# Pole-table products of an S4 convolution: one 96-row group of products, or two 48-row halves in the upper and lower half of the array

## The chip, the cores and the metric

The kernel runs on one core of one Trainium2 chip. The metric is the device time of one execution in microseconds; lower is better. The times shown are medians over several executions of the same program. The profile is one execution taken by the hardware profiler; its span runs from the first instruction to the last.

## The reference

The reference is a block of two mixers on 2048 tokens of 576 channels: an S4 state-space convolution, then a gated MLP with a spatial product. Both are wrapped in adaptive layer norm. What matters here is how the convolution's kernel K comes about, from 128 complex poles for each channel:

```python
dt = jnp.exp(log_dt)[:, None]
A = A_re + 1j * A_im
Bc = B_re + 1j * B_im
Cc = C_re + 1j * C_im
logdA = dt * A
dB = dt * Bc
P = jnp.exp(logdA[:, :, None] * l[None, None, :])
K = jnp.einsum("dn,dnl,dn->dl", Cc, P, dB).real
...
y = irfft(rfft(u padded) * rfft(K padded)) + u * Dskip
...
x = x + ga * y                       # first mixer, on the layer norm of x
x = x + gb * gMLP(layernorm(x) ...)  # second mixer
```

So for each channel and pole a power of exp(dt A) is needed at 2048 positions l, weighted by C dB and summed over the poles. (The lines with the transforms are written shorter here.)

## The kernel before, in words

**Powers as products of tables.** A position is split as l = a + 32 b. A power is then a table over 32 values of a times a table over 64 values of b. Log magnitude and phase of each table entry are linear in the pole's parameters, so TensorE makes them: the parameters of 16 channels, each split into three bf16 parts, stand as the rows of a stationary operand (`lb`, `lc`, `la`), and constant selection rows (`sel`) stream past. Its columns are 16 channels x 32 positions, 512 for one product. `lb` holds the log magnitudes: 3 parts of alpha and 3 of the log weight, times 16 channels, 96 rows. `lc` holds 3 parts of the phase step tau, 48 rows. `la` holds 3 parts of 64 tau (taken modulo 1) and 3 of the phase offset, 96 rows. The 128 output partitions are the poles.

**Groups and ticks.** The 576 channels are 36 groups of 16, `g`, in four chunks of nine. The loop at lines 650 to 714 has 40 ticks; a tick works on several groups at different steps of a pipeline:

- `e_unit` (lines 416 to 426): two products into a `ps` buffer (two PSUM banks, two such buffers) and one into a `pk` bank (four of those), then ScalarE's Exp on each (lines 423 and 426). It is issued for three groups at a time, in every third tick. The table `et` has five buffers.
- `t_unit` (428 to 438): two products into a `ps` buffer, `lc` (line 432) and `la` (433). ScalarE adds a large constant, which rounds (434); VectorE subtracts to get the phase modulo 1 (435) and takes its absolute value (437).
- `s_unit` (440 to 443), one tick later: ScalarE's two Sins, cosine and sine.
- `p_unit` (445 to 459), two ticks later: VectorE's five products of magnitudes with cosines and sines.
- `kg_unit` (461 to 471), three ticks later: 32 small products sum over the poles, and ScalarE copies the result into `kab`; `d_unit` adds the skip term; `k1_unit` (477 to 492), a tick later, takes the first step of K's transform, and ScalarE or VectorE copies it out.

From tick 11 on the same ticks also carry the transform of the input and the product with K's transform: `u_unit` (523 to 532; ScalarE copies `ue`), `z_unit` (534 to 543), `v_unit` (545 to 552; ScalarE copies `v`), and `y_unit` (587 to 597). In ticks 0 to 7 they carry the layer norm and the first step of the input's transform (`ln_unit`, 393 to 408), which uses `ps` buffers too. Behind the ticks come the second norm and the gMLP, whose instructions are mostly recorded at line 140.

**Exp and Sin.** The two functions are not in one table set of ScalarE; where one follows the other the program has an ACT_TABLE_LOAD, at the line of the function that needs it. Copies and the rounding need none.

**How the pole parameters get there.** `poles` (188 to 279) works them out on VectorE and ScalarE, chunk 0 first, chunks 1 to 3 together. `split3` (197 to 213) splits each into three bf16 parts and stores them into the DRAM tensors `pa_d`, `pb_d` and `pc_d`, through GpSimd's (POOL's) DMA queue: five stores for a chunk. `poles_load` (283 to 287) reads the three tables of a chunk back, one DMA each, before tick 0 and in ticks 7, 13 and 21.

**What sets the order.** Within the ticks the instructions are not pinned: a list scheduler orders them for each engine when the program is built, by its own estimates, by priority in order of issue, and by which buffers are free. Startup, tick 0's products and everything behind the ticks are pinned to program order.

Of the kernel before, what the change touches and what calls it, by code (L numbers as in the profile page):

```python
# [11 lines left out]
BF = mybir.dt.bfloat16  # L12
# [19 lines left out]
def consts():  # L32
# [51 lines left out]
    eye = np.eye(16)  # L84
    rgt = np.zeros((6, 16, 16, 32))
    rge = np.zeros((6, 16, 16, 32))
    rpe = np.zeros((6, 16, 16, 64))
# [5 lines left out]
    rpt = np.zeros((6, 16, 16, 32))  # L93
# [59 lines left out]
def ssm(tc, I, x1_d, consts_s, dram, mod_d, mlp):  # L153
# [5 lines left out]
    with ExitStack() as ctx:  # L159
# [23 lines left out]
        sel = tb.tile([96, 2560], BF, name="sel", bufs=1)  # L183
# [4 lines left out]
        def poles(c0, c1, Q, own=None):  # L188
# [8 lines left out]
            def split3(*items):  # L197

                n = 3 // (c1 - c0)
                parts = []  # L200
                for i, (src, dst, k) in enumerate(items):
                    if not todo:
                        t_ = ep.tile([128, 3, 432], BF, name="pt")
                        todo.extend(t_[:, :, w * j:w * j + w] for j in range(n))
                    parts.append((src, dst, k, todo.pop(0), t("sq%d" % (i % 2))))
                for src, dst, k, pt, q in parts:
                    A.activation(pt[:, 0], src, AF.Copy)
                    V.tensor_tensor(q, src, pt[:, 0], op=ALU.subtract)
# [11 lines left out]
            def run():  # L220
# [36 lines left out]
                split3((al, pb_d, 0), (tau, pc_d, 0))  # L257
# [3 lines left out]
                split3((tau64, pa_d, 0), (lw, pb_d, 3))  # L261
# [15 lines left out]
                split3((ph, pa_d, 3))  # L277
# [138 lines left out]
        def e_unit(g):  # L416
            c, gi = divmod(g, 9)
            lb = lt["lb", c]
            e = et[g] = tb.tile([128, 1536], F32, name="et", bufs=5)
            pa = ps2()  # L420
            for h in range(2):
                T.matmul(pa[:, h], lb[:, gi], sel[:, 1024 + 512 * h:1536 + 512 * h], start=True, stop=True)
            A.activation(e[:, :1024].rearrange("p (h n) -> p h n", h=2), pa, AF.Exp)
            pb = ps1()
            T.matmul(pb, lb[:, gi], sel[:, 512:1024], start=True, stop=True)
            A.activation(e[:, 1024:], pb, AF.Exp)

        def t_unit(g):
# [3 lines left out]
            T.matmul(pa[:, 0], lt["lc", c][:, gi], sel[:48, 2048:2560], start=True, stop=True)  # L432
            T.matmul(pa[:, 1], lt["la", c][:, gi], sel[:, :512], start=True, stop=True)
# [11 lines left out]
        def p_unit(g):  # L445
# [6 lines left out]
            c3 = ct.rearrange("p x (c j) -> p x c j", c=16)  # L452
            s3 = f.rearrange("p x (c j) -> p x c j", c=16)
# [1693 lines left out]
```

## Time and profile before

| | |
|---|---|
| median of 3 executions | 1782.84 us (1781.9 to 1785.29) |
| the profiled execution | 1788.13 us |
| its span | 1786.3 us |
| mean granted TensorE clock | 0.978 |
| TensorE (PE) busy | 1686.7 us, 94% |
| VectorE (DVE) busy | 1266.6 us, 71% |
| ScalarE (ACT) busy | 854.4 us, 48% |
| GpSimd (POOL) busy | 227.0 us, 13% |

Times in the profile are in microseconds from the span's start, unless they are marked ns. PE is TensorE's products, PEld its weight loads. A row of the timeline has the start, the duration, the engine, the line of the kernel, the operation, the tile written and the tiles read, shapes, and in brackets how long the engine had been idle and what ended that. A row of the windows has one stretch: its length, and each engine's busy time with the number of instructions. A busy PE is not PE at its peak, since products are pipelined and their ends are modelled.

### The profile page before, as it was taken

How to read it: one execution, taken by the hardware profiler on the slowest of the kernel's cores; microseconds unless marked ns; L12 is line 12 of the kernel's file. 1: busy time of each engine (PE TensorE's matmuls, PEld its weight loads, DVE VectorE, ACT ScalarE, POOL GpSimd, SP SyncE). 2: the span in 40 equal slices, each digit the busy share in tenths (PEclk: the TensorE clock that was granted, in tenths of full speed). 3: DMA queues.
4: the chain of work that ended last, by engine and by line, in shares of the span. 5: the costliest groups of instructions: out<-in, count | busy, mean ns of one | idle time of the engine just before them, and what ended most of it. 6: DMA issues, size and time to landing. Idle time of an engine off the chain costs nothing.

```text
span 1786.3 us, 35743 instructions
## 1 busy us (share of the span) xinstructions
PE 1686.7 (94%) x14830; PEld 1255.3 (70%) x14830; DVE 1266.6 (71%) x2331; ACT 854.4 (48%) x1129; POOL 227.0 (13%) x364
## 2 busy tenths in 40 slices
PE   3599899998899999999989999999999999999999
PEld 1355555565455445777878888888888888888887
DVE  6785999966998998688889677688344468344432
ACT  4778999954477666445434444234222224122210
POOL 2111223332122211000000000000111100111100
PEclk9789999998999999999999999999999999999999
DMA  9465646679688779777665886773766573556531
GB/s 268 145 198 179 196 120 167 176 204 304 206 260 266 249 228 264 284 248 250 240 209 164 282 299 233 269 253 118 250 225 226 203 231 100 193 195 215 194 111 40
DMA packets 182193, 377.80 MB, mean 212 GB/s; under 512 B 37680, under 2 KB 101552, under 8 KB 181264
## 3 DMA queue, kind: packets, MB, share of 16 engines
q1 hardware_dynamic: 140000, 177.29, 33.1%
q0 software_dynamic: 36128, 171.57, 28.9%
q10 hardware_dynamic: 5904, 26.67, 3.7%
q8 instruction: 116, 1.90, 0.4%
q14 instruction: 45, 0.37, 0.1%
HBM read 264.73 MB, written 101.31 MB: 205 GB/s over the span
## 4 chain that ended last, share of the span: by engine, by line
PE 58%; DVE 10%; DMA 8%; issue 4%; ACT 1%; POOL 1%; SPq 0%; ACTq 0%; DVEq 0%; POOLq 0%
PE ps L140 54%; DMA zset<-set_d 2%; DMA wsst<-in_w_spT 1%; DVE zset L140 1%; DVE bsz L140 1%; DMA win_d<-wso 1%; DVE n L140 1%; DVE gt L140 1%; DVE rq L140 1%; PE pk L527 1%; ACT z L140 1%; PE pk L540 1%; DMA ue<-v_d 1%; DMA z_d<-z 1%; DVE wsp L140 1%
## 5 line engine op out<-in xcount | busy, mean ns | idle before, releaser
L140 PEld LDWEIGHTS <-zset 128*128 128x128 f16 x7182 | 702.8, 98 | 95.3 <-DVE zset L140 9.5
L140 PE MATMUL ps<-wsp,zset 128*128 128x256 f16 x6048 | 669.2, 273 | 9.1 <-DVE zset L140 7.5
L140 PE MATMUL pz<-wz,nt 128*128 128x512 f16 (+1 forms) x1120 | 222.5, 358 | 12.3 <-ACT nt L140 5.3
L140 ACT ACTIVATE z<-gt 128x1024 f16<-128x1024 f32 x56 | 59.0, 1054 | 285.4 <-DVE gt L140 285.4
L140 PEld LDWEIGHTS <-nt 128*128 128x128 f16 x1120 | 108.7, 98 | 119.9 <-ACT nt L140 6.9
L140 DVE SCALAR_TENSOR_TENSOR gt<-ps,sc,bsp 128x512 f32<-128x512 f32 x36 | 27.0, 750 | 206.0 <-PE ps L140 204.3
L140 PE MATMUL ps<-wout,z 128*128 128x288 f16 x1344 | 170.0, 286 | 0.0
L1855 POOL DMA_DIRECT2D zset<-set_d x96 | 50.9, 530 | 872.0 <-PE ps L140 626.1
L140 PEld LDWEIGHTS <-z 128*128 128x128 f16 x1344 | 131.5, 98 | 33.0
L140 DVE TENSOR_TENSOR raw<-raw 128x512 f32<-128x512 f32 (+2 forms) x228 | 119.1, 528 | 13.0 <-DMA raw<-z_d 8.7
L140 PE MATMUL ps<-n2o,zset 128*128 128x256 f16 x1134 | 128.2, 273 | 0.0
L140 DVE SCALAR_TENSOR_TENSOR gt<-ps,sc,gt 128x512 f32<-128x512 f32 (+1 forms) x180 | 122.2, 696 | 7.6
L140 ACT ACTIVATE zset<-raw 128x1792 f16<-128x1792 f32 x48 | 81.2, 1691 | 60.8 <-PE ps L140 27.0
L140 DVE TENSOR_TENSOR zset<-raw,zset 128x1792 f16<-128x1792 f32 x48 | 97.0, 2020 | 15.6 <-ACT zset L140 15.6
L140 DVE TENSOR_TENSOR z<-ps,z 128x512 f32<-128x512 f32 (+1 forms) x126 | 72.0, 599 | 36.8 <-ACT z L140 26.7
L140 ACT ACTIVATE wsp<-raw,sc 128x1792 f16<-128x1792 f32 x25 | 44.6, 1784 | 42.7 <-DVE raw L140 35.0
L140 ACT ACTIVATE z<-z,sc 128x1024 f32<-128x1024 f32 x21 | 24.1, 1148 | 75.6 <-DVE z L140 71.9
L435 DVE SCALAR_TENSOR_TENSOR ft<-ft,ps 128x1024 f32<-128x1024 f32 x36 | 43.8, 1217 | 18.0 <-ACT ft L434 18.0
L140 ACT ACTIVATE z<-z,nm,r 128x1152 f32<-128x1152 f32 x24 | 31.4, 1341 | 51.6 <-DVE nm L140 29.5
L140 ACT ACTIVATE z<-pz,sc 128x512 f32<-128x512 f32 (+1 forms) x96 | 51.6, 583 | 9.2 <-PE pz L140 4.6
L140 PE MATMUL ps<-n2q,wf 128*128 128x512 f16 x252 | 55.7, 379 | 0.0
L140 PE MATMUL ps<-wout,z1b 128*128 128x288 f16 x384 | 52.4, 286 | 0.0
(361 smaller groups left out, 2512.0 us busy)
## 6 DMA issues: line engine op xcount, KB each, us to landing
zset<-set_d POOLq DMA_DIRECT2D x96, 896.0 KB, 5.0
raw<-z_d SPq DMA_DIRECT2D x48, 512.0 KB, 5.6
set_d<-zset ACTq DMA_DIRECT2D x24, 896.0 KB, 6.1
z_d<-z POOLq DMA_DIRECT2D x32, 576.0 KB, 9.4
zset<-wa_d POOLq DMA_DIRECT2D x18, 896.0 KB, 4.9
raw<-in_w_spT SPq DMA_DIRECT2D x25, 512.0 KB, 4.5
set_d<-zset SPq DMA_DIRECT2D x12, 896.0 KB, 5.2
u_d<-st1o POOLq DMA_DIRECT2D x16, 576.0 KB, 3.8
```

The source lines that it names most:

```text
L140: return self.tc.keep_in_program_order(f(*a, **k))
L435: V.scalar_tensor_tensor(f, f, MAGIC, pa, op0=ALU.subtract, op1=ALU.subtract)
L527: T.matmul(pm, fwd, u1, start=True, stop=True)
L540: T.matmul(pm[:, w * j:w * j + w], cst[k // 8][:, k % 8], k1t[c][:, k, :w], start=True, stop=True)
L1855: self.nc.gpsimd.dma_start(o, self.set_d[f, j - 1] if j else self.wa_d[f])
```

## The change

A group's 16 channels are split into two halves of eight. The rows of a half, 6 x 8 = 48, stand on partitions 0 to 47 or 64 to 111 of the stationary tiles and of `sel`, so that one half's product runs on the array's upper rows and the other's on its lower rows, each with a PSUM bank of its own. `lc` becomes a 48-row half as well: it is read from `pa_d`, which now holds tau, 64 tau and the offset in nine rows, and the rows of 64 tau meet zeros in `sel`. `pc_d` is gone.

In `e_unit` three products of 512 columns become two of 512 and two of 256, and the second pair goes into a second `ps` buffer, where a `pk` bank was used. In `t_unit` two products of 512 columns become four of 256, each written into runs of 32 columns. Its tables then lie in another order, and `p_unit` reads cosines and sines in runs of 32 elements. Each store of the split parameters becomes two DMAs, and each load too.

```diff
@@ consts
-    eye = np.eye(16)
+    eye = np.eye(8)
...
-    sel = np.concatenate([rgt.reshape(96, 512), rge.reshape(96, 512), rpe.reshape(96, 1024), rpt.reshape(96, 512)], axis=1)
+    half = np.concatenate([rgt.reshape(48, 256), rge.reshape(48, 256), rpe.reshape(48, 512), rpt.reshape(48, 256)], axis=1)
+    sel = np.zeros((112, 1280))
+    sel[:48] = sel[64:] = half
@@ ssm
-        pa_d = dram.tile([4, 6, CW], BF, name="pa_d")
-        pb_d = dram.tile([4, 6, CW], BF, name="pb_d")
-        pc_d = dram.tile([4, 3, CW], BF, name="pc_d")
+        pa_d = dram.tile([4, 2, 9, CW // 2], BF, name="pa_d")
+        pb_d = dram.tile([4, 2, 6, CW // 2], BF, name="pb_d")
...
@@ split3
-                        Q.dma_start(dst[c, k:k + 3].rearrange("q (p f) -> p q f", p=128), pt[:, :, 144 * (c - c0):144 * (c - c0) + 144])
+                        for h in range(2):
+                            Q.dma_start(dst[c, h, k:k + 3].rearrange("q (p f) -> p q f", p=64),
+                                        pt[64 * h:64 * h + 64, :, 144 * (c - c0):144 * (c - c0) + 144])
...
@@ poles_load
-            for n, d_, k in (("lb", pb_d, 6), ("lc", pc_d, 3), ("la", pa_d, 6)):
-                t_ = tb.tile([16 * k, 9, 128], BF, name=n)
-                Q.dma_start(t_, d_[c].rearrange("q (c g n) -> (q c) g n", c=16, g=9))
+            for n, d_, k in (("lb", pb_d, 0), ("lc", pa_d, 0), ("la", pa_d, 3)):
+                t_ = tb.tile([112, 9, 128], BF, name=n)
+                for h in range(2):
+                    Q.dma_start(t_[64 * h:64 * h + 48], d_[c, h, k:k + 6].rearrange("q (c g n) -> (q c) g n", c=8, g=9))
                 lt[n, c] = t_
+
+        def rows(c0, w):
+            return [sel[64 * h:64 * h + 48, c0:c0 + w] for h in range(2)]
+
+        def halves(t, gi):
+            return [t[64 * h:64 * h + 48, gi] for h in range(2)]
@@ e_unit
-            pa = ps2()
-            for h in range(2):
-                T.matmul(pa[:, h], lb[:, gi], sel[:, 1024 + 512 * h:1536 + 512 * h], start=True, stop=True)
+            pa, pb = ps2(), ps2()
+            for h, (l, r) in enumerate(zip(halves(lb, gi), rows(512, 512))):
+                T.matmul(pa[:, h], l, r, start=True, stop=True)
+            for h, (l, r) in enumerate(zip(halves(lb, gi), rows(256, 256))):
+                T.matmul(pb[:, h, :256], l, r, start=True, stop=True)
             A.activation(e[:, :1024].rearrange("p (h n) -> p h n", h=2), pa, AF.Exp)
-            pb = ps1()
-            T.matmul(pb, lb[:, gi], sel[:, 512:1024], start=True, stop=True)
-            A.activation(e[:, 1024:], pb, AF.Exp)
+            A.activation(e[:, 1024:].rearrange("p (h n) -> p h n", h=2), pb[:, :, :256], AF.Exp)
@@ t_unit
-            T.matmul(pa[:, 0], lt["lc", c][:, gi], sel[:48, 2048:2560], start=True, stop=True)
-            T.matmul(pa[:, 1], lt["la", c][:, gi], sel[:, :512], start=True, stop=True)
+            for k, (n, c0) in enumerate((("lc", 1024), ("la", 0))):
+                for h, (l, r) in enumerate(zip(halves(lt[n, c], gi), rows(c0, 256))):
+                    T.matmul(pa[:, h].rearrange("p (c k j) -> p k c j", c=8, k=2)[:, k], l, r, start=True, stop=True)
@@ p_unit
-            c3 = ct.rearrange("p x (c j) -> p x c j", c=16)
-            s3 = f.rearrange("p x (c j) -> p x c j", c=16)
+            c3, s3 = [x.rearrange("p h (c k j) -> p k (h c) j", c=8, k=2) for x in (ct, f)]
```

More of the change, by code (lines that the diff above doesn't have):

```diff
@@ L83, in consts @@
         st3b[rows, 1::2] = tr
-    eye = np.eye(16)
-    rgt = np.zeros((6, 16, 16, 32))
-    rge = np.zeros((6, 16, 16, 32))
-    rpe = np.zeros((6, 16, 16, 64))
+    eye = np.eye(8)
+    rgt = np.zeros((6, 8, 8, 32))
+    rge = np.zeros((6, 8, 8, 32))
+    rpe = np.zeros((6, 8, 8, 64))
     rgt[:3] = eye[None, :, :, None] * a
@@ L92, in consts @@
     rpe[:3] = eye[None, :, :, None] * b
-    rpt = np.zeros((6, 16, 16, 32))
+    rpt = np.zeros((6, 8, 8, 32))
     rpt[:3] = eye[None, :, :, None] * (np.arange(32) + 0.5)
-    sel = np.concatenate([rgt.reshape(96, 512), rge.reshape(96, 512), rpe.reshape(96, 1024), rpt.reshape(96, 512)], axis=1)
+    half = np.concatenate([rgt.reshape(48, 256), rge.reshape(48, 256), rpe.reshape(48, 512), rpt.reshape(48, 256)], axis=1)
+    sel = np.zeros((112, 1280))
+    sel[:48] = sel[64:] = half
     ones = np.zeros((128, 128))
@@ L182, in ssm @@
         tb = tabs.enter_context(tc.tile_pool(name="tb", reuse_waits="tile", bufs=2))
-        sel = tb.tile([96, 2560], BF, name="sel", bufs=1)
+        sel = tb.tile([112, 1280], BF, name="sel", bufs=1)
         dsk = tb.tile([128, 144], F32, name="dsk", bufs=1)
@@ L256, in run @@
                 yield
-                split3((al, pb_d, 0), (tau, pc_d, 0))
+                split3((al, pb_d, 0), (tau, pa_d, 0))
                 yield
@@ L260, in run @@
                 V.tensor_tensor(lw, lw, ldt, op=ALU.add)
-                split3((tau64, pa_d, 0), (lw, pb_d, 3))
+                split3((tau64, pa_d, 3), (lw, pb_d, 3))
                 yield
@@ L276, in run @@
                 V.tensor_tensor(ph, ph, rnd, op=ALU.subtract)
-                split3((ph, pa_d, 3))
+                split3((ph, pa_d, 6))
             return run()
```

## The prediction, made before the changed kernel was run

> **What bounds the kernel now.** I read the page's slices first, to see where the touched code runs. The products of the pole tables belong to ticks 0 to 35, between 44 and 365 us of the 1786.3 us span, slices 2 to 8 of 40.
>
> ```profile
> PE   3599899998899999999989999999999999999999
> DVE  6785999966998998688889677688344468344432
> ACT  4778999954477666445434444234222224122210
> ```
>
> In slices 5 to 8 all three engines stand at 9: whichever gets more work there makes the kernel longer. Averages hide which one has room, so next I asked for the stretches between the starts of the Exp bursts in the full ticks (each burst serves three ticks; columns: PE, weight loads, DVE, ACT, POOL busy, granted clock, DMA share, GB/s).
>
> ```profile
> 189.36:212.44 23.08, 22.80 (x311) 12.79 (x311) 21.34 (x33) 22.52 (x30) 6.76 (x12) 1.00 0.72 202
> 212.44:235.86 23.42, 22.67 (x309) 12.93 (x306) 21.64 (x34) 21.89 (x29) 6.39 (x11) 1.00 0.37 108
> 235.86:257.13 21.27, 20.75 (x293) 11.99 (x293) 19.10 (x30) 21.01 (x28) 4.80 (x8) 1.00 0.33 91
> 257.13:281.42 24.29, 23.54 (x325) 13.87 (x322) 23.61 (x37) 21.88 (x28) 8.72 (x15) 1.00 0.60 173
> 281.42:303.79 22.37, 21.85 (x309) 12.77 (x309) 19.86 (x30) 21.30 (x27) 5.43 (x9) 1.00 0.57 155
> 303.79:328.93 25.14, 24.39 (x341) 14.76 (x338) 23.80 (x38) 21.91 (x29) 8.03 (x13) 1.00 0.62 173
> 328.93:355.21 26.28, 25.76 (x336) 15.02 (x335) 23.77 (x36) 24.59 (x31) 9.02 (x15) 1.00 0.63 176
> sum 165.85, PE 161.75 PEld 94.15 DVE 153.11 ACT 155.11 POOL 49.14; mean PE 23.11 PEld 13.45 DVE 21.87 ACT 22.16 POOL 7.02
> ```
>
> Seven stretches, 21 ticks, 165.85 us. PE is busy 161.75 of them, ACT 155.11, DVE 153.11. So PE sets the pace, but ACT has only 165.85 - 155.11 = **10.74 us** to spare in all 21 ticks, 0.51 us a tick. The third view is the timeline of ACT through one burst and the tick behind it.
>
> ```profile
> 281.42 1.28 ACT L423 ACT_TABLE_LOAD   x1
> 282.72 1.02 ACT L423 ACTIVATE et<-ps 128x1024 f32<-128x1024 f32 x1
> 283.64 0.59 ACT L426 ACTIVATE et<-pk 128x512 f32<-128x512 f32 x1
> 284.11 1.03 ACT L423 ACTIVATE et<-ps 128x1024 f32<-128x1024 f32 x1
> ...
> 286.99 1.11 ACT L434 ACTIVATE ft<-ps,consts_s 128x1024 f32<-128x1024 f32 x1
> 288.12 1.28 ACT L442 ACT_TABLE_LOAD   x1
> 289.42 1.15 ACT L442 ACTIVATE ft<-ft,consts_s 128x1024 f32<-128x1024 f32 x1
> 290.48 1.04 ACT L443 ACTIVATE ft<-ft 128x1024 f32<-128x1024 f32 x1
> 291.42 0.58 ACT L551 ACTIVATE v<-pk 128x512 f32<-128x512 f32 x1
> 291.90 0.64 ACT L471 ACTIVATE kab<-pk 128x256 f32<-128x256 f32 x1
> 292.31 0.66 ACT L528 ACTIVATE ue<-pk 128x512 f32<-128x512 f32 x1
> 292.84 1.12 ACT L434 ACTIVATE ft<-ps,consts_s 128x1024 f32<-128x1024 f32 x1
> ```
>
> A burst costs a table load for Exp (1.28 us), the three units' Exps with no Sin between them, and a table load back for Sin. The steps from start to start are what ACT pays when it never waits: 0.92 us for the wide Exp, 0.47 for the narrow one, about 1.0 for the rounding (L434), 1.06 and 0.94 for the Sins, 0.48, 0.41 and 0.53 for the three copies.
>
> **The change part by part.**
>
> *The order on ACT.* The two Exps of a unit used to read one two-bank `ps` buffer and one `pk` bank; now both read `ps` buffers, of which there are two. Three units in a row therefore need six turns of a ring of two, where they needed three. The scheduler answers to that, and the order in which the instructions stand in the changed program shows how. One letter per ACT instruction, * a table load, E and e the wide and the narrow Exp, t the rounding, s and S the Sins, v g u k copies; six ticks of before, then of after:
>
> ```
> * E e E e E e t * s S v g u k t s S v g u t s S v g u k * E e E e E e t * s S v g u t s S v g u k t s S v g u
> * E e * s * E e * S * E e v g u t k t * s S v g u t s S * E v g u k e E e * s * E e * S t v g u v t s S g u k t s S v g u
> ```
>
> Exp and Sin now alternate inside the burst: six table loads in the first three ticks and four in the next, where there were two and two. Over the whole program I count 58 loads against 32, **26 more**. Of these 20 fall into the seven stretches above (4, 6, 4, 6, 4, 6, 4 = 34 against 14) and 6 into ticks before them; the last burst and the tail have as many as before.
>
> *Full ticks.* 20 x 1.283 us = 25.7 us; 155.11 + 25.7 = 180.8 us of ACT work in stretches that took 165.85. ACT becomes the bound, and the sum without a single wait is +14.9 us. Then I walked by hand through the six ticks with the steps above. In the three-tick group with six loads, the third unit's Exp ends 12.8 us in; the next product on PE needs that buffer and waits some 4 us for it, which costs nothing by itself, since ACT has five instructions of cover. Two roundings then come close together, and the Sin behind them waits for DVE's two steps on the first rounding (1.22 + 0.69 us, with one more in between), about 1.2 us beyond ACT's own time:
>
> ```profile
> 288.14 1.22 DVE L435 SCALAR_TENSOR_TENSOR ft<-ft,ps 128x1024 f32<-128x1024 f32 x1 [2.19 <-ACT ft L434]
> 289.39 0.69 DVE L437 TENSOR_SCALAR ft<-ft 128x1024 int32<-128x1024 int32 x1
> ```
>
> The group with four loads shows no such wait. Three groups of the first kind: 3 x 1.2 = 3.6. **Full ticks: 14.9 + 3.6 = +18.5 us.** Lower end: packed back to back, ACT's steps (with 1.42 us per load, as an instruction ahead of a load does not overlap it) sum to 25.9 and 24.6 us for the two groups, 3 x 25.9 + 4 x 24.6 = 176.1, or +10. Upper end: ACT keeps the idle share that it has now, 180.8 x 165.85 / 155.11 = 193.3, or +27.5.
>
> The Trainium skill has another price: "ScalarE: Activation LUTs", under "What ACT_TABLE_LOAD costs", puts a drain of about 1380 ns on top of 1283 ns, some 2.66 us per switch. Here the load at 281.42 is followed by its Exp at 282.72, 1.30 us on, and no drain shows, so the sum goes by the row.
>
> *Early ticks.* Six more loads, 7.7 us, where ACT has more room.
>
> ```profile
> 55.10:95.20 40.10, 28.02 (x143) 15.31 (x142) 31.08 (x72) 31.55 (x46) 8.68 (x12) 0.73 0.40 131
> 95.20:139.10 43.90, 39.59 (x412) 23.27 (x412) 33.95 (x86) 32.08 (x43) 8.51 (x13) 0.92 0.69 214
> 139.10:164.90 25.80, 21.56 (x301) 13.24 (x300) 16.59 (x28) 23.23 (x32) 4.48 (x7) 1.00 0.44 154
> 164.90:189.36 24.46, 20.38 (x256) 11.16 (x254) 16.97 (x25) 20.72 (x25) 2.07 (x4) 0.72 0.86 258
> ```
>
> ACT is busy 107.6 of 134.3 us, 80%, and no engine is full; the layer norm's products share the `ps` ring. I take half of the 7.7, **+4 us**; the ends are 0, and 14 if all loads show and the ring, now with 12 more turns there, costs another 0.5 us a turn.
>
> *PE.* Per unit before: three 96-row products, then a 48-row and a 96-row one.
>
> ```profile
> 281.13 0.38 PE L425 MATMUL pk<-sel,lb 96*128 96x512 bf16 x1
> 281.35 0.59 PE L422 MATMUL ps<-sel,lb 96*128 96x512 bf16 x2
> ...
> 286.20 0.39 PE L432 MATMUL ps<-sel,lc 48*128 48x512 bf16 x1
> 286.52 0.39 PE L433 MATMUL ps<-sel,la 96*128 96x512 bf16 x1
> ```
>
> Products of one shape step by 0.22 us; where the row count changes the step is 0.32. A unit is 3 x 0.22 + 2 x 0.32 = 1.3 us. After: two of 512 and two of 256 columns, then four of 256, each on half the rows. No row shows two halves side by side. If they run so, a unit is about 0.22 + 0.11 + 0.22 plus two changes of 0.1, 0.75 us, a gain of 0.55; if one after another with every weight load showing (0.1 each, eight), 2.1 us, a loss of 0.8. In 21 ticks that is -11.6 to +16.8, so PE's work is between 150.2 and 178.6 us: below ACT's 180.8 at both ends. I take **0** on the path. The cover is ACT's new work; without that cover PE's gain would be the kernel's.
>
> *DVE and the wider patterns.* Its cosines and sines are now read in runs of 32 elements 64 apart. The nearest rows are a copy into runs 128 elements apart and a product on dense data:
>
> ```profile
> 290.06 0.69 DVE L490 COPY k<-pk 128x512 f32<-128x512 f32 x1
> 290.67 0.68 DVE L454 TENSOR_TENSOR pg<-et,ft 128x512 f32<-128x512 f32 x1
> ```
>
> No difference: **0**.
>
> *DMAs.* Stores of the split poles go from 20 to 40 and loads from 12 to 24, all on POOL's queue, 0.76 and 0.52 us of POOL each. The first tables hurry most:
>
> ```profile
> 26.21 0.52 POOL L140 DMA_DIRECT2D la<-pa_d  x1 [0.55 <-DMA pa_d<-pt]
> ...
> 44.26 1.06 PE L140 MATMUL ps<-sel,lb 96*128 96x512 bf16 x2
> ```
>
> Five more stores and three more loads put at most 5 x 0.76 + 3 x 0.52 = 5.4 us ahead of the last load; the first product starts 18 us behind it, after the modulation's products on PE. **0**, at most 1.
>
> **Sum.** 18.5 + 4 = +22.5 us. The profiled execution took 1788.13 us, 1.83 over its span; the median of the three timed runs is 1782.84, 5.3 us lower, and the addition is carried over to it: 1782.84 + 22.5 = **1805**. Behind tick 36 the transforms, the second norm and the gMLP hang on the last tick, so I pass the delay on undiminished.
>
> **The rivals.**
> - *Packed* (1793): ACT runs back to back and the early loads hide, +10. For it: ACT has work of several ticks queued. Against: the Sins' wait on DVE.
> - *Halves in line* (1811): the two halves don't run side by side, so the change doesn't do what it says. PE at up to 178.6 us is then within 2 us of ACT and the two make each other wait; I put 6 us on it, a third of PE's extra.
> - *ACT keeps its idle share and the ring costs early* (1824): 27.5 + 14 = +41.
> - *PE's gain decides* (1772): faster. PE sets the pace today, and 21 x 0.55 = 11.6 us less of it is 11 us less of kernel, if the 20 loads fit into ACT's 10.74 us of room. That decides at 0.54 us a load; the row has 1.28. A balance in between gives no change (1783).
> - *The skill's drain* (1833): a stall of another 1.38 us behind each load, 20 x 2.66 = 53, less 10.74, +42, and 8 early. The page is the one named above; the rows speak against it.
>
> **How the numbers follow.** Forecast 50%, packed 15%, halves in line 15%, idle share kept 12%, PE's gain 4%, no change 3%, the drain 1%. The range takes in the first four: 1793 to 1824. A measurement here can tell about 0.2%, 3.6 us, from no change: slower 93%, same 3%, faster 4%.
>
> **What would show it.** In the profile after: 26 more table loads, ACT busier by about 33 us in all; ACT at 95% or more in the full ticks, their six-tick period near 52.7 us in place of 47.4; PE below 93% there, waiting for `ps` buffers on the Exps; the pair of half products stepping by one product's time or by two. It is wrong if the full ticks keep their length, or if they grow with ACT idle and PE full.

## The result, and the profile after

| | before | after |
|---|---|---|
| median of 4 executions each | 1784.07 us (1781.9 to 1786.35) | 1824.83 us (1821.32 to 1831.69) |
| ratio after/before | | 1.023 (95%: 1.0212 to 1.0247) |
| the profiled execution, its span | 1788.13, 1786.3 us | 1826.31, 1824.5 us |
| mean granted TensorE clock | 0.978 | 0.964 |

The change costs 40.8 us by the medians. The forecast was +22.5, and the range ended at 1824. The profiled span grew by 38.2 us. After's slices, to lay over those of before:

```profile
PE   4586788899799999999999999999999999999999
DVE  6774778885798999788899777689444469344432
ACT  5767999983567666545544343334222124122110
PEclk8688889999899999999999999999999999999999
```

In slices 5 to 8 ACT stands at 9; PE, which stood at 8 or 9 there before, at 7 and 8. The granted clock (PEclk) is at 6 to 8 in the first six slices.

The second view answers to before's stretches between Exp bursts (columns as there).

```profile
205.67:230.00 24.33, 22.00 (x301) 11.66 (x300) 20.78 (x31) 24.07 (x31) 8.18 (x15) 0.93 0.44 116
230.00:258.56 28.56, 22.33 (x290) 12.27 (x289) 21.06 (x33) 26.49 (x30) 5.13 (x9) 0.82 0.29 82
258.56:283.23 24.67, 22.27 (x323) 12.95 (x322) 21.37 (x32) 24.56 (x31) 4.91 (x9) 1.00 0.35 98
283.23:308.84 25.61, 19.73 (x240) 11.80 (x239) 18.92 (x30) 25.10 (x28) 7.91 (x15) 0.87 0.41 121
308.84:336.42 27.58, 26.30 (x409) 15.39 (x409) 24.35 (x37) 25.87 (x34) 6.86 (x12) 1.00 0.56 162
336.42:362.74 26.32, 21.14 (x256) 12.52 (x253) 19.52 (x31) 25.09 (x28) 5.73 (x10) 0.87 0.47 132
362.74:394.78 32.04, 30.73 (x438) 17.96 (x437) 28.05 (x43) 29.02 (x38) 10.06 (x18) 1.00 0.62 175
sum 189.11, PE 164.50 PEld 94.56 DVE 154.05 ACT 180.19 POOL 48.77; mean PE 23.50 PEld 13.51 DVE 22.01 ACT 25.74 POOL 6.97
```

189.11 us where before had 165.85: **+23.3**. ACT is busy 180.19 us, 95% of it, and idle 8.9; PE was idle 4.1 us and is now idle 24.6. The groups with six loads (the second, fourth and sixth row) run at a clock of 0.82 to 0.87, and the work that PE does not get done there comes later: in the last group PE is the full engine (30.73 of 32.04).

The same view for the ticks ahead of them, cut at the first products or bursts that answer to before's cuts.

```profile
53.61:94.27 40.66, 26.54 (x156) 15.42 (x155) 33.73 (x79) 29.02 (x45) 13.81 (x22) 0.73 0.42 138
94.27:142.71 48.44, 42.24 (x480) 25.75 (x482) 33.34 (x84) 34.58 (x45) 7.65 (x12) 0.89 0.59 182
142.71:178.71 36.00, 22.98 (x306) 14.75 (x307) 16.52 (x26) 30.28 (x36) 5.99 (x10) 0.80 0.35 119
178.71:205.67 26.96, 18.95 (x229) 11.47 (x230) 15.56 (x23) 23.04 (x28) 2.77 (x5) 0.70 1.05 304
sum 152.06, PE 110.72 PEld 67.40 DVE 99.16 ACT 116.92 POOL 30.23; mean PE 27.68 PEld 16.85 DVE 24.79 ACT 29.23 POOL 7.56
```

Before took 134.26 us from its first rounding (55.10) to its first full burst (189.36); after takes 152.06: **+17.8**. More than half of it is in the third row, which begins with a burst: 36.00 in place of 25.80 us, or 34.92 if the row ends, as before's does, at the next burst's table load (177.63). ACT is not full there, PE is busy 64%, DVE 46%, and the clock is 0.80 where it was 1.00. In the four rows together PE idles 41.3 us where it idled 24.7, and its waits for an Exp to free a `ps` buffer add up to 14.5 us where before had 0.4. The three longest kinds in after (us in total, times, longest):

```profile
PE ps L432 <- ACT et L435: 4.9, 3, 4.0
...
PE ps L415 <- ACT et L435: 4.3, 1, 4.3
...
PE ps L444 <- ACT et L435: 2.8, 1, 2.8
```

The start-up is 1.5 us shorter and what is behind the ticks 1.4 us: 17.8 + 23.3 - 1.5 - 1.4 = 38.2.

**One early burst on two engines.** ACT first. The same burst of before began at 139.13 and its last Exp ended at 144.75, 5.6 us.

```profile
142.71 1.28 ACT L435 ACT_TABLE_LOAD   x1
144.01 1.02 ACT L435 ACTIVATE et<-ps 128x1024 f32<-128x1024 f32 x1
144.93 0.59 ACT L436 ACTIVATE et<-ps 128x512 f32<-128x512 f32 x1
145.54 1.28 ACT L453 ACT_TABLE_LOAD   x1
146.83 1.15 ACT L453 ACTIVATE ft<-ft,consts_s 128x1024 f32<-128x1024 f32 x1
148.00 1.28 ACT L435 ACT_TABLE_LOAD   x1
149.29 1.02 ACT L435 ACTIVATE et<-ps 128x1024 f32<-128x1024 f32 x1
...
153.19 1.28 ACT L435 ACT_TABLE_LOAD   x1
154.48 1.02 ACT L435 ACTIVATE et<-ps 128x1024 f32<-128x1024 f32 x1
155.40 0.59 ACT L436 ACTIVATE et<-ps 128x512 f32<-128x512 f32 x1
```

It now takes 142.71 to 155.99, 13.3 us: two Sins and four more loads stand between the Exps. ACT is never idle in it. PE, in the same time:

```profile
140.93 0.28 PE L444 MATMUL ps<-sel,lc 48*128 48x256 bf16 x2
141.05 0.27 PE L444 MATMUL ps<-sel,la 48*128 48x256 bf16 x2
...
141.74 0.39 PE L432 MATMUL ps<-sel,lb 48*128 48x512 bf16 x2
...
144.04 0.28 PE L434 MATMUL ps<-sel,lb 48*128 48x256 bf16 x2
...
145.08 0.39 PE L432 MATMUL ps<-sel,lb 48*128 48x512 bf16 x2 [0.18 <-ACT et L435]
145.57 0.28 PE L434 MATMUL ps<-sel,lb 48*128 48x256 bf16 x2
...
150.37 0.61 PE L432 MATMUL ps<-sel,lb 48*128 48x512 bf16 x2 [4.05 <-ACT et L435]
150.85 0.39 PE L434 MATMUL ps<-sel,lb 48*128 48x256 bf16 x2
155.56 0.40 PE L415 MATMUL ps<-gsp,cs 96*128 96x288 bf16 x1 [4.31 <-ACT et L435]
155.75 1.16 PE L416 MATMUL ps<-ln_x,rt 128*128 128x288 f32 x2
...
161.34 0.65 PE L416 MATMUL ps<-ln_x,rt 128*128 128x288 f32 x2
```

The third unit's product stands idle 4.05 us for the buffer that ACT's Exp at 149.29 frees, and the layer norm's product behind it 4.31 us for the next one. No other product runs on PE in either wait. The granted clock falls from 1.00 to 0.50 at 147.3 us, in the first wait, 0.9 us after PE's last product: the wide pair takes 0.61 us at 150.37 where it took 0.39 at 145.08. It is back at 1.00 at 160.9, 5.3 us after the products go on; until then the layer norm's pair takes 1.16 us in place of 0.65. The Trainium skill, "TensorE: Matmul & The Clock Gate", section "What's actually happening", says that the clock falls to half after an idle window of about 3.4 us and comes back after a busy one. The trace agrees in kind, but not in the time: here 0.9 us without a product come before the fall.

The loads by line, in after's first 460 us, and what waited longest in its seven full stretches:

```profile
L435 ACT ACT_TABLE_LOAD x25 | 32.1, 1283 | 0.4
L453 ACT ACT_TABLE_LOAD x16 | 20.5, 1283 | 0.3
L454 ACT ACT_TABLE_LOAD x10 | 12.8, 1283 | 0.2
```

```profile
PE ps L444 <- ACT et L435: 14.5, 4, 4.4
...
DVE et L466 <- ACT ft L454: 8.9, 4, 2.4
```

58 loads in the whole program against 32, as the order had shown. PE's four waits are of phase products (L444) that want the buffer of an Exp: 4.42 us in each of the three six-load groups, and one of 1.25. DVE's four are for Sins that come late. One of PE's, and what PE does after it:

```profile
242.84 0.40 PE L444 MATMUL ps<-sel,lc 48*128 48x256 bf16 x2 [4.42 <-ACT et L435]
...
246.36 2.08 PE L559 MATMUL pk<-za,small 128*128 128x512 f32 x2
...
254.87 1.02 PE L559 MATMUL pk<-za,small 128*128 128x512 f32 x2
```

Held 4.42 us, then 2.08 us for a pair that takes 1.02 at 254.87. The granted clock is 0.50 from 239.4 to 249.7.

### The profile page after: what moved, and what is told of

It reads as the page before. It is cut to its first block, busy times and chain, and to the rows that moved or that the text cites. A ratio compares the mean times of both kernels' runs of the same rounds, so it can differ in the third digit from the quotient of the medians.

```text
span 1824.5 us, 36040 instructions
## 1 busy us (share of the span) xinstructions
PE 1688.5 (93%) x14938; PEld 1257.4 (69%) x14938; DVE 1268.5 (70%) x2331; ACT 889.2 (49%) x1155; POOL 239.4 (13%) x396
## 4 chain that ended last, share of the span: by engine, by line
PE 57%; DVE 11%; issue 4%; DMA 4%; ACT 1%; POOL 1%; ACTq 0%; POOLq 0%; DVEq 0%
PE ps L142 53%; PE pz L142 2%; DMA zset<-set_d 2%; DVE bsz L142 1%; DVE zset L142 1%; DVE n L142 1%; DVE rq L142 1%; DMA z_d<-z 1%; DVE gt L142 1%; DVE wsp L142 1%; ACT z L142 1%; DVE nt L142 0%; DVE rx L142 0%; DVE wso L142 0%; DVE z L142 0%
```

## The experiments

Two questions: which part of the change costs the time (the halves on PE, or the sixth turn of the `ps` ring), and by which way a table load of 1.28 us becomes more. The table puts the runs side by side. A burst runs from its first wide Exp, with the table load where one stands directly ahead of it, to the end of its last Exp, read from ACT's timeline and added up over the three early bursts (those of ticks 3, 6 and 9) and over the seven full ones. A narrow Exp that the scheduler has drawn ahead of its burst, with a load of its own, is not counted (before has one at 81.02 us and one at 164.87). "Start" is the start of the first full burst, "stretches" the length of the seven; both are of one profiled execution, which lay 9 us above its kernel's median in e1, 4 above in before and e9, 4.5 below in e10, and within 3 us in the others. The median is that of the kernel, the ratio that to before on the same chip with its 95% interval.

| kernel | loads | early bursts | start | full bursts | stretches | median | ratio |
|---|---|---|---|---|---|---|---|
| before | 32 | 17.6 | 189.36 | 40.8 | 165.85 | 1784.07 | |
| after | 58 | 38.7 | 205.67 | 84.7 | 189.11 | 1824.83 | 1.023 (1.0212 to 1.0247) |
| e1 ring alone | 58 | 42.5 | 209.53 | 86.2 | 191.43 | 1826.06 | 1.0238 (1.0214 to 1.0262) |
| e5 halves, old banks | 34 | 15.0 | 180.96 | 40.6 | 164.37 | 1778.5 | 0.9958 (0.9938 to 0.9977) |
| e4 halves in `t_unit` | 32 | 20.6 | 186.07 | 41.7 | 165.25 | 1784.74 | 0.9994 (0.9979 to 1.0009) |
| e6 after, no loads | 8 | 25.3 | 189.50 | 45.9 | 157.85 | 1775.75 | 0.9942 (0.9926 to 0.9958) |
| e7 before, no loads | 8 | 13.9 | 178.96 | 32.2 | 160.81 | 1774.57 | 0.9929 (0.9912 to 0.9946) |
| e3 loads between the Sins | 58 | 18.4 | 189.69 | 40.3 | 170.67 | 1794.89 | 1.0061 (1.004 to 1.0082) |
| e11 loads in the burst | 54 | 25.3 | 192.97 | 69.7 | 192.21 | 1818.72 | 1.019 (1.0174 to 1.0206) |
| e8 ring early | 40 | 40.4 | 205.87 | 44.8 | 167.20 | 1806.37 | 1.0117 (1.01 to 1.0134) |
| e13 after, tables early | 60 | 36.5 | 201.76 | 85.4 | 195.58 | 1825.35 | 1.0227 (1.0203 to 1.0251) |
| e14 before, tables early | 32 | 17.8 | 182.73 | 40.8 | 165.82 | 1782.19 | 0.9994 (0.9977 to 1.0011) |
| e9 after, Exps together | 36 | 31.7 | 214.57 | 48.6 | 162.17 | 1807.62 | 1.0122 (1.0103 to 1.0141) |
| e10 before, Exps together | 34 | 25.0 | 192.14 | 39.9 | 162.72 | 1794.2 | 1.0056 (1.0037 to 1.0075) |
| e12 ring late, together | 34 | 15.0 | 184.06 | 48.7 | 163.55 | 1776.49 | 0.995 (0.9934 to 0.9966) |
| e2 halves in `pk` banks | 32 | 16.3 | 189.02 | 41.6 | 193.32 | 1817.96 | 1.0186 (1.0168 to 1.0204) |
| e16 two `pk` turns | 32 | 18.3 | 189.18 | 41.6 | 191.02 | 1809.52 | 1.0145 (1.0119 to 1.0171) |
| e15 e5, tables early | 34 | 15.0 | 182.12 | 40.6 | 164.37 | 1773.77 | 0.9943 (0.9922 to 0.9963) |

### The ring or the halves: e1, e5, e4

e1 is before with the narrow product in a `ps` buffer, so six turns and no halves.

```diff
-            pb = ps1()
+            pb = ps2()[:, 0]
```

> The kernel before with one edit: the narrow product of e_unit goes into a ps buffer in place of a pk bank. No halves, no more DMAs. Its program has 58 table loads, like the changed kernel, and the three-unit Exp burst is cut by Sins in the same way. Theory RING (six turns on a ring of two ps buffers make the loss: the table loads, and PE held behind a waiting product): about the changed kernel's time, 1815 to 1835 us. Theory HALVES (the half products, their weight loads, mode changes or DMAs make the loss): at most a few us over the kernel before, 1784 to 1795.

The whole loss is there, without a single half: +40.6 us by the medians, 58 loads, 20.2 us more ahead of the first full burst and 25.6 in the stretches. The additional turns of the ring are the cause.

e5 is the reverse, after with the halves and the old banks: the two wide half products stay, and the narrow one is one product of all 112 rows (those between the halves hold zeros) into one `pk` bank.

```diff
+                if n == "lb":
+                    G.memset(t_[32:64], 0.0)
...
-            pa, pb = ps2(), ps2()
+            pa = ps2()
...
+            pb = ps1()
+            T.matmul(pb, lb[:, gi], sel[:, 1024:], start=True, stop=True)
+            A.activation(e[:, 1024:], pb, AF.Exp)
```

> The changed kernel with PSUM used as before: the wide products of e_unit and all products of t_unit in halves, but the narrow one is one product over all 112 rows (the 16 between the halves are zero) into one pk bank. Three ps turns and three pk turns per burst, 34 table loads (two more than before). The DMAs are those of the changed kernel. Theory TURNS (any additional turn of a PSUM ring in the burst holds PE, the halves themselves cost nothing): 1778 to 1790 us. If halves or DMAs had a price of their own: over 1795.

Faster than before by 0.4%. Its window over the seven stretches:

```profile
180.96:345.33 164.37, 154.19 (x2242) 91.53 (x2242) 153.13 (x232) 154.69 (x200) 49.11 (x81) 1.00 0.53 150
```

PE is busy 154.19 us in place of 161.75: the halves do take 7.6 us of work off it. The stretches get only 1.5 us shorter; the rest of the gain is ahead of them.

e4 has the halves in `t_unit` alone (the parameter tables `la` and `lc` and their stores and loads as in the change, `lb` as before):

```diff
-            T.matmul(pa[:, 0], lt["lc", c][:, gi], sel[:48, 2048:2560], start=True, stop=True)
-            T.matmul(pa[:, 1], lt["la", c][:, gi], sel[:, :512], start=True, stop=True)
+            for k, (n, c0) in enumerate((("lc", 256), ("la", 0))):
+                for h, (l, r) in enumerate(zip(halves(lt[n, c], gi), rows(c0, 256))):
+                    T.matmul(pa[:, h].rearrange("p (c k j) -> p k c j", c=8, k=2)[:, k], l, r, start=True, stop=True)
```

> Halves in t_unit alone: lc and la as in the changed kernel, lb, its three 96-row products and its buffers as before. 32 table loads. RING: no loss; PE loses 0.64 us a unit and gets 0.24 to 0.45 back into its place, so 1774 to 1785 us. HALVES: a good part of the loss, 1795 or more.

PE's busy time falls to 156.79 us, and the time does not change. Relief on PE alone is worth little here, though PE was the busiest engine.

### Without the loads: e6, e7

Both kernels with Exp in place of both Sins; the cosines and sines are thereby left out.

```diff
-            A.activation(ct, ct, AF.Sin, bias=halfpi, scale=-TWO_PI)
-            A.activation(f, f, AF.Sin, scale=-TWO_PI)
+            A.activation(ct, ct, AF.Exp, bias=halfpi, scale=-TWO_PI)
+            A.activation(f, f, AF.Exp, scale=-TWO_PI)
```

> The changed kernel with Exp in place of Sin in s_unit (so the cosines and sines are left out, and numbers of the same size stand in their place): no table load is needed in the ticks. The ring of two ps buffers has six turns per burst as in the changed kernel. To be read against the kernel before with the same edit (e7). LOADS: the ring hurts because table loads between its turns stretch the burst, so without loads the two kernels are within 8 us of each other. TURNS: the six turns hold PE by themselves, and 20 us or more stay between the two.

> The kernel before with Exp in place of Sin in s_unit (cosines and sines left out in the same way): 24 fewer table loads, 31 us less ACT work. Every theory: PE is as full as before, so the gain is far below 31 us; 1765 to 1785 us.

1775.75 against 1774.57: without the loads 1.2 of the 40.8 us are left. But e6 has the halves, which were worth 8 us in e5, and its first full burst starts 10.5 us later than e7's. So the six turns alone may cost up to some 9 us; these two runs do not separate that from the halves. That delay is not PE waiting for the ring's Exps: ahead of the full ticks it waits 2.0 us in all for Exps in `ps` in e6, 3.3 in e7. In the stretches e6 is shorter than e7, with the same six turns as after.

### Where a load stands decides what it costs: e3, e11

e3 is before with a one-column Exp between the two Sins of every third group, which gives the second Sin its bias; for that the two Sins change places, and a constant holds the logarithm of pi/2. It brings as many loads as the change, but no turn of a ring, and outside the bursts.

```diff
-            A.activation(ct, ct, AF.Sin, bias=halfpi, scale=-TWO_PI)
             A.activation(f, f, AF.Sin, scale=-TWO_PI)
+            hp = halfpi
+            if g % 3 == 1:
+                hp = tb.tile([128, 1], F32, name="hp")
+                A.activation(hp, f[:, 0, :1], AF.Exp, scale=0.0, bias=consts_s[:, 3:4])
+            A.activation(ct, ct, AF.Sin, bias=hp, scale=-TWO_PI)
```

> The kernel before, with a one-column Exp between the two Sins in every third tick; its result is the constant that the second Sin takes as its bias. 58 table loads, the same 26 more as the changed kernel, but no product has to wait for a ps buffer longer than before. If the table loads by themselves are the whole loss: about 1825 us. If they are the part that the prediction priced (ACT full, PE's waits free): 1800 to 1812, clock about 0.98 as before. The difference to the changed kernel is then PE's waiting for buffers and its lower clock.

```profile
189.69:360.36 170.67, 161.62 (x2167) 91.86 (x2167) 151.75 (x228) 169.84 (x218) 41.66 (x75) 1.00 0.48 136
```

ACT is busy 169.84 of 170.67 us, 99.5%. Its room of 10.74 us is used up and the rest shows: 14 more loads cost 4.8 us, 0.34 each, at a full clock. The ten early ones cost 0.3 us together. By the medians all 26 cost 9.4 us, 0.36 each. The arithmetic of the prediction's floor would give 14 x 1.283 - 10.74 = 7.2 us for the 14, and one Sin pair, some 2 us of ACT, has left this window: it is about right, on the high side. The time, 1794.89, is even below the 1800 to 1812 that was expected for loads priced that way.

e11 is before with a one-column Sin between the second and third unit's Exps, whose result the third unit's wide Exp takes as bias. Three turns of `ps`, one of `pk`, but two loads within the burst.

```diff
+            zb = {}
+            if g > 2 and g % 3 == 2:
+                z = tb.tile([128, 1], F32, name="hp")
+                A.activation(z, et[g - 1][:, 1535:1536], AF.Sin, scale=0.0)
+                zb = {"bias": z}
-            A.activation(e[:, :1024].rearrange("p (h n) -> p h n", h=2), pa, AF.Exp)
+            A.activation(e[:, :1024].rearrange("p (h n) -> p h n", h=2), pa, AF.Exp, **zb)
```

> The kernel before with a one-column Sin (of 0) between the second and the third unit's Exps of each burst but the first; the third wide Exp takes it as its bias. 54 table loads, 22 more, all inside the bursts, but three ps turns per burst as before. If it is enough that loads stand inside the burst: 1810 us or more. If PE must also be waiting for the buffer that comes free behind them: near the kernel with the loads between the Sins (1795), 1790 to 1803.

The view that PE must also be kept from its `ps` buffer, 1790 to 1803, falls: it is 1818.72. The seven stretches of e11, and its longest waits on PE, PEld and DVE in them:

```profile
192.97:385.18 192.21, 172.43 (x2202) 98.36 (x2200) 155.03 (x232) 176.17 (x220) 46.41 (x80) 0.95 0.44 127
```

```profile
PEld pk L545 <- ACT v L556: 14.6, 5, 3.5
DVE pg L459 <- ACT ft L447: 13.8, 7, 2.9
PE pk L545 <- ACT v L556: 12.9, 5, 3.2
DVE ft L440 <- ACT ft L439: 12.1, 7, 2.9
```

As many loads as cost 4.8 us between the Sins, 14, cost 26.4 inside the burst, 1.9 us each, and ACT is idle 16 us. (ACT also has more to do, 21.1 us with the small Sins, which is 10.3 beyond its room; the idling is the rest. By the medians the 22 loads cost 34.0 us, 1.5 each.) Each burst is 4.1 us longer and each stretch 3.8: nearly all of the delay comes through. What stands behind the burst on ACT comes late: the rounding and the Sins, for which DVE waits seven times each, and the `v` copy, for which PE waits, up to 3.2 us at a time.

### The early ticks: e8, e13, e14

e8 is before with six turns up to group 14 only, that is in all bursts up to and with the first full one.

```diff
-            pb = ps1()
+            pb = ps2()[:, 0] if g < 15 else ps1()
```

> The kernel before with the narrow product of e_unit in a ps buffer for the first 15 groups alone (the bursts of ticks 0 to 9), a pk bank from there on: 40 table loads, 8 more than before, all ahead of the full ticks. If the early ticks lose by products held behind a burst that table loads stretch: 14 to 20 us over before, 1798 to 1808. If by the loads' own time: 5 us or less.

```profile
54.30:205.87 151.57, 116.76 (x1135) 67.75 (x1135) 99.12 (x208) 117.32 (x150) 24.43 (x36) 0.79 0.55 175
```

The first full burst starts at 205.87 us, as in after (205.67), with six more loads ahead of it (the other two stand in that burst); the stretches are back near before's. So the early 17.8 and the later 23.3 us are two separate losses. ACT is idle 34 of these 151.57 us, and PE waits 10.6 us for Exps in `ps`. Loads alone don't do that: e11 has two more loads inside each of the three early bursts, but three turns, and starts 3.6 us later than before, with 1.8 us of such waits. Nor do six turns without loads: in e6 these waits are 2.0 us.

One way for the early loss stood in the trace: the tables of chunk 1 are loaded in tick 7 on POOL's queue, behind the layer norm's last stores, which wait for its held products. Before issued that load at 160.01 us; after issues it at 173.43, and PE then waits 4.37 us for it. e13 and e14 are after and before with this load in tick 5.

```diff
-            if tick in (7, 13, 21):
+            if tick in (5, 13, 21):
```

> The changed kernel, with the three tables of chunk 1 loaded in tick 5 instead of tick 7. In the changed kernel that load is issued at 173.43 us (before: 160.01), directly behind the last store of the layer norm on the same queue, and the first product of group 9 waits for it. QUEUE (the early loss goes from the lengthened burst through the layer norm's products and stores to this load): most of the 13.4 us by which the load is late disappears, first full burst near 193 to 198 instead of 205.67, full ticks unchanged near 189, time 1810 to 1817. Rival WORK (the early ticks themselves are that much longer, and the load is late only because everything is): at most 3 us, time 1820 or more.

> The kernel before with the same move of the load. Its first product of group 9 waits 2.35 us for lb. QUEUE: a gain of 2 to 6 us, 1778 to 1782, much less than in the changed kernel. WORK: no difference, within 2 us of before. If it gains as much as the changed kernel does, the load was as much on the path before, and it isn't what the change made late.

In e13 the load is issued 32 us earlier, but the layer norm behind it is held all the same (the row with 14.96 us of waiting for ACT):

```profile
141.52 1.04 POOL L142 DMA_DIRECT2D lb<-pb_d  x2
...
159.63 0.74 POOL L418 DMA_DIRECT2D u_d<-st1o  x1 [14.96 <-ACT st1o L417]
```

The first full burst comes 3.9 us earlier, the stretches take 6.5 us longer with two more loads, and the time is the same. My theory of the queue falls: the load was late because the ticks were. In e14 the first full burst comes 6.6 us earlier, and the time, 2.7 us less by the medians, is within its interval of no change; it lies just outside both expectations.

### Exps kept together: e9, e10, e12

e9 is after with the Exps and Sins pinned to program order on ACT, e10 before with the same.

```diff
+        AP = mlp.tied.scalar
...
-            A.activation(e[:, :1024].rearrange("p (h n) -> p h n", h=2), pa, AF.Exp)
+            AP.activation(e[:, :1024].rearrange("p (h n) -> p h n", h=2), pa, AF.Exp)
...
-            A.activation(ct, ct, AF.Sin, bias=halfpi, scale=-TWO_PI)
-            A.activation(f, f, AF.Sin, scale=-TWO_PI)
+            AP.activation(ct, ct, AF.Sin, bias=halfpi, scale=-TWO_PI)
+            AP.activation(f, f, AF.Sin, scale=-TWO_PI)
```

> The changed kernel with the Exps of e_unit and the Sins of s_unit pinned to program order on ACT, so no Sin comes between the three units of a burst: 36 table loads, six turns of the ring as in the changed kernel. LOADS: most of the 41 us goes, 1785 to 1800 us. TURNS: PE waits for the ring all the same, 1810 us or more.

> The kernel before with the Exps and Sins pinned to program order, the control for e9: same PSUM use as before, 34 table loads. e9 lost its 21 us ahead of the full ticks (its full ticks are shorter than before's). If the pinning did that: 1800 us or more here too. If the ring did: 1780 to 1790.

e9 (1807.62 us) and e10 (1794.2) each fall between their two expectations; the pinning by itself makes the kernel before 0.6% slower. With the Exps together the full stretches take 162.17 us with six turns, less than before's 165.85. All that e9 loses, it loses early: 25.2 us by the first full burst, though it has hardly more loads than e10, which loses 2.8. There ACT stands and waits where after's ACT does Sins and loads. That the early ticks pay either way for six turns of two buffers that the layer norm uses as well is my reading; no run takes the layer norm out of the ring.

e12 puts the two together: e5 up to group 14, from group 15 on six turns as in the change with the Exps pinned (the Sins from group 12).

```diff
+            if g < 15:
...
+                pb = ps1()
+                T.matmul(pb, lb[:, gi], sel[:, 1024:1536], start=True, stop=True)
...
+            pb, AP = ps2(), mlp.tied.scalar
...
+            AP.activation(e[:, 1024:].rearrange("p (h n) -> p h n", h=2), pb[:, :, :256], AF.Exp)
```

> Ahead of the full ticks the kernel of e5 (wide halves, narrow product in one pk bank); from group 15 on the changed kernel's e_unit, with six turns of the ps ring per burst, but Exps (from group 15) and Sins (from group 12) pinned to program order, so that the Exps of a burst stay together. 34 table loads. LOADS (the ring hurts only where table loads come between its turns): as e5, 1773 to 1787 us. TURNS: 1795 or more.

1776.49 us, 0.5% faster than before, with 163.55 us in the stretches. Six turns cost nothing in the full ticks if the Exps stay together.

### A detour: e2, e16, e15

e2 is after with the two narrow halves in a `pk` bank each, and an Exp for each.

```diff
-            pa, pb = ps2(), ps2()
+            pa, pb = ps2(), [ps1(), ps1()]
...
-                T.matmul(pb[:, h, :256], l, r, start=True, stop=True)
+                T.matmul(pb[h][:, :256], l, r, start=True, stop=True)
...
+            for h in range(2):
+                A.activation(e[:, 1024 + 256 * h:1280 + 256 * h], pb[h][:, :256], AF.Exp)
```

> The changed kernel with one edit: the two 256-column products of e_unit go into two pk banks, with an Exp of 256 columns for each, and the ps ring is left with three turns per burst as before. 32 table loads. RING: the loss is gone, 1772 to 1790 us: the halves save PE some 0.5 us a unit, and 36 more small Exps cost ACT about 0.2 us each, 7 us. HALVES: 1805 or more.

A miss. The table loads are back at 32 and the early loss is gone, yet the stretches take 27.5 us longer. e16 has the two `pk` turns in before, with no halves:

```diff
-            pb = ps1()
-            T.matmul(pb, lb[:, gi], sel[:, 512:1024], start=True, stop=True)
-            A.activation(e[:, 1024:], pb, AF.Exp)
+            pb = [ps1(), ps1()]
+            for h in range(2):
+                T.matmul(pb[h][:, :256], lb[:, gi], sel[:, 512 + 256 * h:768 + 256 * h], start=True, stop=True)
+            for h in range(2):
+                A.activation(e[:, 1024 + 256 * h:1280 + 256 * h], pb[h][:, :256], AF.Exp)
```

> The kernel before with the narrow product of a unit in two 96-row products of 256 columns, each in a pk bank of its own, with an Exp each; no halves. It has the turns of the pk ring that e2 has. PK (the loss of e2 comes from the second pk turn and the fifth Exp instruction): the loss is there without halves, 1808 to 1822, nearly all of it in the full ticks, with 32 table loads. Rival HALVES (the loss of e2 comes from the half products): within 6 us of before.

```profile
189.18:380.20 191.02, 176.12 (x2216) 103.33 (x2211) 155.09 (x233) 161.29 (x220) 43.52 (x80) 0.91 0.47 133
```

The loss is there without halves. No engine is full in it: PE 92%, ACT 84%, DVE 81%. The bursts are about as short as before's. So the second `pk` turn, or the additional Exp, costs 25 us with no more table loads; which of the two was not tried. What it shares with the change is the hold: PE waits seven times for an Exp to free a `ps` buffer, 11.4 us in all (before 1.6), and the clock is 0.91. In the burst at 216.35 us the wait is 2.32 us, and the granted clock is 0.50 from 218.4 to 225.3.

That goes for the whole table. In the six kernels whose stretches take over 20 us longer than before's (after, e1, e13, e11, e2, e16) the mean clock in them is 0.89 to 0.95, in all others 0.99 or 1.00. Waits of PE of over 2 us in the stretches occur in those six alone, and in or right behind each the clock falls; in the others no wait is longer than 1.54 us.

e15 is e5 with the tables in tick 5 (the edit of e13).

> The halves in the old banks (e5, 1778.5) with the same move of the load. There the load is issued from 137.48 to 154.28, ahead of where it is before. QUEUE: the load is no longer what ends the early ticks, 0 to 4 us less than e5, 1774 to 1779. WORK: the same as e5 within 2.

1773.77 us, the fastest median of the study. The intervals of e5, e12 and e15 overlap; all three beat both kernels, before by 0.4 to 0.6%.

## Why the prediction came out too low

**Right: what the change does to ACT, and what it doesn't do elsewhere.** The order gave 26 more loads, 20 of them in the stretches, and they are there. ACT's floor in the full ticks was worked out as 180.8 us; it is 180.19. The halves run side by side: two of 256 columns start 0.12 us apart (140.93 and 141.05 each stand for a pair), and e5's PE has 7.6 us less work. DVE is busy 154.05 us against 153.11, and its products on cosines and sines take the same time each (0.69 and 1.22 us), so the strided reads cost nothing. The start-up with its additional DMAs is 1.5 us shorter, not longer. Behind the ticks the delay comes through but for 1.4 us.

**The step that failed: a product held on PE for a `ps` buffer was priced at nothing.** For the full ticks the words are "the next product on PE needs that buffer and waits some 4 us for it, which costs nothing by itself, since ACT has five instructions of cover". For the early ticks the forecast took half of the loads' own time and nothing for the 12 more turns. The wait itself was foreseen (4.42 us at 242.84). It was priced by whether ACT runs dry during it, and ACT hardly does. But the products of other groups come only after the waiting one; none runs on PE in the meantime. They then run at half the clock, and what ACT and DVE need of them comes later. e11 shows what a lengthened burst costs by itself: 3.8 us a stretch for 4.1 us of burst. e3 shows that as many loads cost 0.34 us each where PE is not held for long (at most 1.1 us for an Exp).

**Early ticks: +4 forecast, 14 as upper end, +17.8 measured.** This is the larger miss, 13.8 us. I took six loads of 1.28 us and asked how many of them ACT's idle 20% would hide; by e3 most of that is hidden. What isn't hidden is that the three early bursts go from 17.6 to 38.7 us and that PE waits for them: 14.5 us for Exps in `ps`, where before had 0.4. e8 gives 16.5 of the loss from the ring alone. The upper end allowed 0.5 us for each of 12 turns; the one burst of tick 6 shows 4.05 + 4.31 us of hold and then 5.3 us of products at half clock. Chunk 1's tables, which I had not looked at there, are not the cause (e13).

**Full ticks: +18.5 forecast, +23.3 measured, within the ends of 10 and 27.5.** The floor is right; the waits were under-priced. ACT is idle 8.9 us in place of the 3.6 that I gave it, and not where I put it: the Sins wait 0.8 us for VectorE in all seven stretches, not 1.2 in each six-load group. The three six-load groups sum to 28.56 + 25.61 + 26.32 = 80.5 us, where the prediction's own steps with that wait give 3 x (25.9 + 1.2) = 81.3. The miss is in the other four, 108.6 us against 4 x 24.6 = 98.4: PE comes out of the six-load groups with work left over, and in the last group it is fuller than ACT (30.73 against 29.02 of 32.04 us). One reading at the start is off by a digit: in slice 5 PE stands at 8, not at 9; nothing hangs on it.

**The rivals.** That ACT keeps its idle share and the ring costs early (27.5 + 14 = 41, 12%) came nearest in time, but by luck: measured are 23.3 + 17.8, and its two parts miss by some 4 us each, in opposite directions. Packed is refuted by the 8.9 us of idle ACT. Halves in line is refuted by their 0.12 us steps, and that PE's gain decides by the slower time. "Without that cover PE's gain would be the kernel's" was wrong: in e5 the cover is gone, PE has 7.6 us less to do, and the stretches gain 1.5. The likely reason, not tested by itself, is that ACT (154.69) and DVE (153.13) stand as high as PE (154.19) and each waits for the other two. The Trainium skill's drain behind each load ("ScalarE: Activation LUTs", "What ACT_TABLE_LOAD costs") does not show either: at 2.66 us a load the 14 in e3 would take 37 us, and those stretches had 10.74 us of room and grew by 4.8.

**Still open.** How the loss after a hold divides between the waiting itself and the half clock: no run holds PE for over 2 us in the full ticks without the clock falling. What six turns cost early with no load at all: e6 and e9 put something there, each with another thing changed as well. Why e2 and e16 hold PE longer than before, with bursts of nearly the same length.

## What to carry to other kernels

A buffer taken from another ring changes the order of the instructions on the engine that empties it; read that order, and where a stretch that others wait behind gets longer, charge the lengthening to the kernel and not only the instructions' own time against that engine's idle share. A wait of TensorE is not free because another engine still has work: what stands behind it on TensorE comes late, and here it came back from such waits at half speed. When a part of a change costs more than the change is worth, take the parts apart: here the halves are worth 0.4% (e5) and the bank for them cost 2.4% (e1).

## What the runs showed of the hardware that I had not expected

- **A hold of PE costs it again afterwards.** In the two holds of tick 6 (4.05 and 4.31 us) the granted clock falls to 0.50, and for 5.3 us behind them a pair of products takes 1.16 us in place of 0.65; after 4.42 us a pair takes 2.08 in place of 1.02. A hold of 2.32 us was enough in e16. Six-load groups ran at a mean clock of 0.82 to 0.87.
- **A table load's price depends on its place**: 0.34 us between the Sins (e3), 1.9 us inside a burst (e11, with the small Sin that brings it), for an instruction of 1.28 us.
- **With three engines busy 92 to 98% of the stretches, less work on the busiest gains little.** 7.6 us less work on PE gave 1.5 us (e5), in `t_unit` alone 5.0 us less gave 0.6 (e4).
